# Nyström attention with two MoE layers on one core: low parts and input sums move from GpSimd to VectorE, and the output products of the rests come first

## The chip, the cores and the metric

The kernel runs on one core of a Trainium2 chip. The metric is the device time of one execution in microseconds (us). Its engines run side by side and wait for each other by semaphores: TensorE (PE in the rows, PEld for its weight loads), VectorE (DVE), ScalarE (ACT), GpSimd (POOL) and SyncE (SP), which here only issues DMAs. PSUM holds the matmuls' outputs in eight banks of 128x512 fp32; SBUF holds the rest.

## The reference

```
A, Bm, C = softmax(q k_lm'), softmax(q_lm k_lm'), softmax(q_lm k')      # 32 landmarks
Z = Bm' / (norm1(Bm) norminf(Bm) + 1e-6);  six times: Z = 2 Z - Z Bm Z
x = A Z C v                                    # (4, 8, 576, 64) -> 2304 x 512
x = (silu(x wg1) * (x wv1)) wo1                # layer 1
out = (sigmoid(x wg2) * (x wv2)) wo2           # layer 2; wg, wv 512 x 1536, wo 1536 x 512
```

The weights come as 64-bit floats, and the kernel converts their raw words to fp32.

## The kernel before

Every fp32 product is done as three products of parts: an operand is split in a high part (a cast to fp32r on ScalarE) and a low part (a subtraction on VectorE, line 366), and the pairs high-high, low-high and high-low (TERMS) are summed in PSUM. Both MoE layers go through the 1536 hidden columns in six chunks of 256 (c = 0 to 5).

Layer 2 is where the change lies; it takes the span from about 447 us on. Its tokens are worked in two steps: step 1 takes 512 tokens of each of batches 0 and 1, step 2 those of batches 2 and 3, and the "rests", 64 tokens of each batch (256 in all), go with step 1. In a step the product of inputs and a chunk of wg and wv is done in 2x2 blocks (two batches, two halves of 256 input columns, two halves of the chunk) with seven block products in place of eight. For these there are

- input sums s1 to s4 of the blocks (`x_blocks`, lines 612 to 615) with high and low parts xl, once for each step;
- weight differences: tile tf, four differences of weight blocks from tiles st (line 408, GpSimd), stored in DRAM for step 2 (wtd), and tile wt, the high part (line 422, ScalarE) and the low part (line 423) of tf. There are two of each for a chunk (j = 0 and 1), one for each half of 128 rows. In step 2 tf and st are loaded, not computed;
- `pair_steps`: the products n = 1, 2, 6, 7, 5, 3, 4 for gate (g) and value (v), six matmuls 128x512 for each (three for each j), in banks `gv` and `n`. `copy` brings a bank to SBUF (ScalarE), `add` adds another (VectorE). `finish` makes h of a quarter: sigmoid on ScalarE, product and low part on VectorE, high part on ScalarE. Products 6, 7, 5 and 4 read wt; products 1, 2 and 3 read wk, the split weights themselves;
- `rest_steps`: the same for the rests by plain products (pgr, pvr with 256 columns, 48 matmuls for a chunk), into tile hy;
- `o2_steps`: the output products of the chunk before, po2_c_i_t for batch i and 128 tokens from t (i = 4 means the rests), six matmuls each, added into oacc by VectorE (line 740; at c = 0 copied by ScalarE, line 738). Their banks have the tags `o` and `a`, two each.

The loop from line 834 runs output products of the chunk before, then the rests, then the pair, in the order in which the generators are called by `run`; after every step `wfill` emits two steps of the weights of the next chunk (raw load on SP, conversion in four operations on ScalarE and VectorE, lines 329 to 338, split, differences, wt, and wo for the output). Each engine works its own list in order; the lists are made by a scheduler that goes by the order of the code and by priorities (`tc.high_priority`). A tile's number of buffers (`bufs`) says how many of a tag are there at once; a new one waits until the last reader of the oldest is done. The tile wt has one buffer for each j, so wt of the next chunk can be cast only when product 4 has read the present one.

Of the kernel before, what the change touches and what calls it, by code (L numbers as in the profile page):

```python
# [16 lines left out]
def nystrom_moe_kernel(tc, q, k, v, wg1, wv1, wo1, wg2, wv2, wo2, out):  # L17
# [371 lines left out]
    def in_weights(layer, c, j):  # L389
        st = [late["w2"].tile([P, 2, FC], F32, tag="st", name=f"st{layer}_{c}_{kh}{j}", bufs=2) for kh in range(2)]  # L390
        wt = [late["w2"].tile([P, 4, 2, P], F32, tag="tf", name=f"tf{layer}_{c}_{j}", bufs=2)]
        for kh in range(2):
            if layer == 1:
                i = PIECES.index((layer, c, load_in, 2 * kh + j))
                load_to(i + 3)
                yield from convert(loaded[i], st[kh])
                WKD[c, kh, j] = dram.tile([P, 2, FC], F32, tag=f"wkd{c}_{kh}{j}", name=f"wkd{c}_{kh}{j}")
                nc.sync.dma_start(WKD[c, kh, j], st[kh])
            else:
                nc.sync.dma_start(st[kh], WKD[c, kh, j])  # L400
            w = WK[c, kh, j] = late["w2"].tile([P, 2, 2, FC], F32R, tag="wk", name=f"wk{layer}_{c}_{kh}{j}", bufs=4)
            split(flat(w[:, 0]), flat(w[:, 1]), flat(st[kh]))
            yield
        t = wt[0]
        if layer == 1:
            b11, b12, b21, b22 = (st[kh][:, :, P * ft:P * ft + P] for kh in range(2) for ft in range(2))
            for o, x, y in ((0, b12, b11), (2, b22, b12), (1, b22, t[:, 0]), (3, b21, t[:, 1])):
                nc.gpsimd.tensor_tensor(t[:, o], x, y, op=ALU.subtract)  # L408
            WTD[c, j] = dram.tile([P, 4, 2, P], F32, tag=f"wtd{c}_{j}", name=f"wtd{c}_{j}")
            nc.sync.dma_start(WTD[c, j], t)  # L410
        else:
            nc.sync.dma_start(t, WTD[c, j])
        yield
        WTF[layer, c, j] = t
        if (layer, c, j) != (1, 0, 1):
            t_split(layer, c, j)
            yield

    def t_split(layer, c, j):
        w = WT[c, j] = late["l2" if j else "w2"].tile([P, 2, 4, 2, P], F32R, tag="wt", name=f"wt{layer}_{c}_{j}", bufs=1)  # L420
        hi, lo, t = (x.rearrange("p t g n -> p (t g n)") for x in (w[:, 0], w[:, 1], WTF[layer, c, j]))
        nc.scalar.copy(hi, t)  # L422
        nc.gpsimd.tensor_tensor(lo, t, hi.bitcast(F32), op=ALU.subtract)  # L423

# [122 lines left out]
    def o1_steps(c, b):  # L547
# [20 lines left out]
        for dm in range(4):  # L568
# [18 lines left out]
            else:  # L587
                if c == NFC - 2:
                    XA.append(p1r.tile([P, HS], F32, tag="h", name=f"xa{dm}", bufs=8)[:, 0:NR * B])
                for bb in range(B):  # L590
# [9 lines left out]
    def x_blocks(step_, x):  # L600


        hi = [AH[:, s, NR:] for s in range(16)]
        eng = nc.gpsimd if step_ == 1 else nc.vector
        for j in range(2):
# [5 lines left out]
            s1, s2, s3, s4 = (new(f"s{n}", F32, "xs") for n in range(1, 5))  # L611
            eng.tensor_tensor(s1, a21, a22, op=ALU.add)
            eng.tensor_tensor(s3, a11, a21, op=ALU.subtract)
            eng.tensor_tensor(s2, s1, a11, op=ALU.subtract)
            eng.tensor_tensor(s4, a12, s2, op=ALU.subtract)
            for n, at, src, home in ((1, 0, a11, "CL"), (2, 8, a12, "CL"), (4, 9, a22, "CL"), (5, 2, s1, "CL"),
# [16 lines left out]
    def w_block(c, n, j, a, gv):  # L633
# [4 lines left out]
        return WT[c, j][:, a, {5: 0, 6: 1, 7: 2, 4: 3}[n], gv]  # L638

    def finish(key, gate, val, g_tile, hi, lo):  # L640
        nc.scalar.activation(g_tile, gate, AF.Sigmoid)
        nc.vector.tensor_tensor(g_tile, g_tile, val, op=ALU.mult)
        split(hi, lo, g_tile)
        H2[key] = (hi, lo)

    def pair_steps(step_, c):
# [15 lines left out]
        def copy(n, gv):  # L662
            t = cp[n, gv] = tmp(f"c{n}{'gv'[gv]}_{nm_}")
            nc.scalar.copy(t, bank[1, gv])  # L664

        def add(n, gv):
            nc.vector.tensor_tensor(cp[n, gv], cp[n, gv], bank[2, gv], op=ALU.add)

# [7 lines left out]
        for gv in range(2):  # L676
            copy(1, gv)
            add(1, gv)
        done(0, 0, 1)
        for gv in range(2):  # L680
# [11 lines left out]
        yield  # L692
        done(1, 1, 5)
        prod(3, 1)
        finish((1, 0), bank[1, 0], bank[1, 1], tmp(f"g12_{nm_}"), *h_pair(1, 0))
        yield
        for gv in range(2):
            prod(4, gv)
            add(6, gv)
            yield  # L700
        done(0, 1, 6)

# [112 lines left out]
    def run(g, n=100, nw=2):  # L815
        for _ in range(n):
# [4 lines left out]
            step(wfill, nw)  # L821

    need(1, 0, 3)
    g2 = pair_steps(1, 0)
    run(g2, 4)
    need(0, NFC - 1, 5)
    emit(f"O{NFC - 1}{B - 1}", 2)
    emit(f"O{NFC - 1}{B}", 2)
    p1r.release()
    late["l2"] = pool("l2", side="right")  # L830
    t_split(1, 0, 1)
    late["hy"] = late["l2"].tile([P, 2 * MT], F32R, tag="hy", name="hy")
    prev = None
    for st in (1, 2):
        for c in range(NFC):
# [4 lines left out]
            if prev:  # L840
                need(*prev, 5)
                o2 = o2_steps(*prev, (0, 1) if prev[0] == 2 else (0, 1, 2) if prev[1] == NFC - 1 else (0, 2, 1))
            if (st, c) == (1, NFC - 1):
# [7 lines left out]
            run(o2, 10 if (st, c) == (2, 0) else 4 if st == 2 else 6)  # L851
            if 0 < c < NFC - 1:
                run(rest)
            need(st, c, 3)
            if prev:
                g2 = pair_steps(st, c)
                run(g2, 4)
            run(o2, 1)
            run(g2, 4)
            run(o2, 1)  # L860
            run(g2, 2)
            run(o2, 1)
            run(g2, 1)
            run(o2)
# [42 lines left out]
```

## Time and profile before

| | |
|---|---|
| median of 3 runs | 943.1 us (941.05 to 944.53) |
| profiled execution | 946.08 us, span 944.3 us |
| TensorE busy | 868.2 us (92%), 6172 matmuls |
| VectorE busy | 675.8 us (72%) |
| ScalarE busy | 472.1 us (50%) |
| GpSimd busy | 174.9 us (19%), 61.8 of them line 423 |
| TensorE's granted clock, mean | 0.965 |

The span is what the trace covers; the execution's own time is 1.8 us longer. All rows below are from this one execution. A row of TensorE's timeline gives the start and the time of a group of matmuls that follow each other, and in brackets the idle time in front of it with the engine and line that ended it; matmuls overlap, so a single 128x512 is shown with some 0.4 us though they follow each other faster.

### The profile page before, as it was taken

The numbers are of one execution on the slowest core, as the hardware profiler recorded it, in microseconds if no ns is written. First come the engines' busy times: TensorE is split into PE (matmuls) and PEld (weight loads), VectorE is DVE, ScalarE is ACT, GpSimd is POOL, SyncE is SP. The second block draws the span as 40 slices with busy tenths as digits, with TensorE's granted clock in tenths as the row PEclk, the third lists the DMA queues.
The fourth block names the chain that finished last, engine by engine and source line by source line (L and its number), as shares of the span: only waits on it lengthen the run. The fifth ranks groups of instructions, "written<-read, shape, count | busy, mean of one in ns | idle before, by whom it ended". The sixth has DMA issues, their size and how long they took to land.

```text
span 944.3 us, 15946 instructions
## 1 busy us (share of the span) xinstructions
PE 868.2 (92%) x6172; PEld 712.6 (75%) x6172; DVE 675.8 (72%) x1227; ACT 472.1 (50%) x967; POOL 174.9 (19%) x170
## 2 busy tenths in 40 slices
PE   5698999999999999989798898989898898988997
PEld 4486868897888888779587786868687676866876
DVE  4979768669767776886856778786869757567555
ACT  5676555457534533563447645444463555534431
POOL 5434330000000000312313322222202022022020
PEclk9899999999999999989999999999998999989999
DMA  8766211024211210451106333434325423122003
GB/s 263 201 207 175 83 37 26 9 83 144 89 37 45 90 46 1 133 180 45 44 11 220 122 128 105 141 112 146 112 84 187 131 90 111 39 96 67 23 1 89
DMA packets 41484, 93.31 MB, mean 99 GB/s; under 512 B 5824, under 2 KB 8896, under 8 KB 41408
## 3 DMA queue, kind: packets, MB, share of 16 engines
q1 hardware_dynamic: 39680, 89.94, 30.4%
q10 hardware_dynamic: 1728, 2.36, 1.0%
q8 instruction: 48, 0.79, 0.3%
q14 instruction: 28, 0.23, 0.1%
HBM read 72.88 MB, written 19.40 MB: 98 GB/s over the span
## 4 chain that ended last, share of the span: by engine, by line
PE 74%; DVE 14%; ACT 4%; issue 3%; DMA 2%; POOL 1%; SPq 1%; DVEq 0%; ACTq 0%; POOLq 0%
PE po L65 28%; PE pg L65 18%; PE pv L65 17%; DVE h L366 3%; PE pu L65 2%; DVE cv L334 2%; PE pvr L65 2%; PE pgr L65 1%; PE tp L148 1%; DMA raw<-in_moe_w_val_dram 1%; PE nw L65 1%; DVE wk L366 1%; DVE xl L366 1%; DVE wo L366 1%; PE as L65 1%
## 5 line engine op out<-in xcount | busy, mean ns | idle before, releaser
L65 PE MATMUL po<-wo,h 128*128 128x512 f32 x432 | 124.5, 429 | 23.5 <-DVE h L366 23.5
L65 PEld LDWEIGHTS po<-wo,h 128*128 128x128 f32 x432 | 87.9, 207 | 49.5 <-DVE h L366 27.4
L423 POOL TENSOR_TENSOR wt<-tf,wt 128x1024 fp32r<-128x1024 f32 x24 | 61.8, 2592 | 284.2 <-ACT wt L422 284.2
L65 PE MATMUL po<-h,wo 128*128 128x512 f32 (+1 forms) x480 | 104.3, 373 | 2.0 <-DVE acc L580 2.0
L65 PEld LDWEIGHTS po<-h,wo 128*128 128x128 f32 x480 | 82.8, 188 | 28.9 <-issue 8.4
L65 PE MATMUL pg<-AH,uw 128*128 128x288 f32 x552 | 96.2, 302 | 1.3 <-ACT uw L365 1.2
L65 PE MATMUL pv<-AH,uw 128*128 128x288 f32 x552 | 93.4, 300 | 3.3 <-ACT sg L526 2.8
L740 DVE TENSOR_TENSOR oacc<-po,oacc 128x512 f32<-128x512 f32 x90 | 60.7, 686 | 45.1 <-PE po L65 44.6
L65 PEld LDWEIGHTS pv<-AH,uw 128*128 128x128 f32 x552 | 80.5, 191 | 7.7 <-ACT sg L526 3.7
L65 PEld LDWEIGHTS pg<-AH,uw 128*128 128x128 f32 x552 | 81.3, 191 | 6.4 <-issue 2.5
L334 DVE SCALAR_TENSOR_TENSOR cv<-cv,cv 128x512 uint32<-128x512 uint32 x84 | 76.1, 911 | 6.9 <-ACT cv L332 6.9
L329 ACT ACTIVATE cv<-raw 128x512 f32<-128x512 f32 x84 | 56.8, 678 | 40.2 <-DMA raw<-in_moe_w_val_dram 14.0
L408 POOL TENSOR_TENSOR tf<-st 128x256 f32<-128x256 f32 x12 | 10.7, 895 | 307.6 <-PE pu L65 240.3
L65 PE MATMUL pv<-AH,wt 128*128 128x512 f32 x192 | 61.9, 403 | 2.7 <-ACT c1v L664 2.7
L65 PE MATMUL pg<-AH,wt 128*128 128x512 f32 x192 | 61.3, 401 | 3.0 <-ACT c1g L664 2.4
L65 PE MATMUL po<-hh,wo 128*128 128x288 f32 x256 | 59.0, 310 | 0.0
L580 DVE TENSOR_TENSOR acc<-po,acc 128x512 f32<-128x512 f32 x64 | 43.8, 687 | 19.3 <-PE po L65 19.0
L332 ACT ACTIVATE cv<-raw 128x512 uint32<-128x512 uint32 x84 | 55.4, 668 | 0.6 <-DVE wo L366 0.6
L526 ACT ACTIVATE sg<-pg 128x288 f32<-128x288 f32 x64 | 26.1, 409 | 46.3 <-PE pg L65 46.3
L65 PEld LDWEIGHTS pv<-AH,wt 128*128 128x128 f32 x192 | 37.2, 194 | 12.1 <-ACT c1v L664 3.1
L65 PEld LDWEIGHTS pg<-AH,wt 128*128 128x128 f32 x192 | 36.6, 191 | 11.6 <-ACT c1g L664 2.6
L365 ACT CAST h<-h 128x288 fp32r<-128x288 f32 x64 | 27.5, 434 | 35.6 <-DVE h L527 35.6
(196 smaller groups left out, 1876.0 us busy)
## 6 DMA issues: line engine op xcount, KB each, us to landing
raw<-in_moe_w_out_dram SPq DMA_DIRECT2D x36, 512.0 KB, 4.1
raw<-in_moe_w_gate_dram SPq DMA_DIRECT2D x48, 128.0 KB, 2.9
raw<-in_moe_w_val_dram SPq DMA_DIRECT2D x48, 128.0 KB, 2.9
raw<-in_moe_w_gate_dram SPq DMA_DIRECT2D x24, 256.0 KB, 3.1
raw<-in_moe_w_val_dram SPq DMA_DIRECT2D x24, 256.0 KB, 3.5
wkd<-st SPq DMA_DIRECT2D x24, 256.0 KB, 2.2
wtd<-tf SPq DMA_DIRECT2D x12, 512.0 KB, 3.0
st<-wkd SPq DMA_DIRECT2D x24, 256.0 KB, 2.7
```

What stands on the lines that cost most here:

```text
L65: return nc.tensor.matmul(o, l, r, start=start, stop=stop, skip_group_check=True)
L148: nc.tensor.transpose(ps[:, j], flat(src[:, 2 * u:2 * u + 2]), ident)
L329: nc.scalar.activation(t0, hiw.bitcast(F32), AF.Copy, scale=2.0 ** -112)
L332: nc.scalar.activation(u1, low, AF.Copy, scale=0.875 * 2.0 ** -29, bias=0.49)
L334: nc.vector.scalar_tensor_tensor(u1, u0, 3, u1, op0=ALU.logical_shift_left, op1=ALU.bitwise_or)
L365: nc.scalar.copy(hi, x)
L366: nc.vector.tensor_tensor(lo, x, hi.bitcast(F32), op=ALU.subtract)
L408: nc.gpsimd.tensor_tensor(t[:, o], x, y, op=ALU.subtract)
L423: nc.gpsimd.tensor_tensor(lo, t, hi.bitcast(F32), op=ALU.subtract)
L526: nc.scalar.activation(sg, pss[0], AF.Silu)
L580: nc.vector.tensor_tensor(sl, ps, sl, op=ALU.add)
L740: nc.vector.tensor_tensor(acc, ps, acc, op=ALU.add)
```

## The change

- `t_split`: the low part of wt is computed on VectorE, not on GpSimd, and tf has one buffer, not two.
- `x_blocks`: the sums of step 1 go to VectorE as well, as those of step 2 did.
- The tile xa lies in another pool, so that p1r is released ahead of the first pair, and wt 0_1 is split ahead of the last output products of layer 1.
- `finish`, `copy` and `add` get a higher priority (100) in the scheduler; `pair_steps` has one more yield, and h of the quarter 1_1 is finished after product 4, not between the two products 3.
- Order: in step 1 the output products go rests, batch 0, batch 1 (2, 0, 1) where they went (0, 2, 1); the rests' products of c = 0 run ahead of the rest of the pair; the four output products of the batch that comes last are spread over the pair as before, but for the last of them, which stood between the two products 3 and now stands behind product 4.

```
-        wt = [late["w2"].tile([P, 4, 2, P], F32, tag="tf", name=f"tf{layer}_{c}_{j}", bufs=2)]
+        wt = [late["w2"].tile([P, 4, 2, P], F32, tag="tf", name=f"tf{layer}_{c}_{j}", bufs=1)]
...
         nc.scalar.copy(hi, t)
-        nc.gpsimd.tensor_tensor(lo, t, hi.bitcast(F32), op=ALU.subtract)
+        nc.vector.tensor_tensor(lo, t, hi.bitcast(F32), op=ALU.subtract)
...
-                    XA.append(p1r.tile([P, HS], F32, tag="h", name=f"xa{dm}", bufs=8)[:, 0:NR * B])
+                    XA.append(late["x"].tile([P, NR * B], F32, tag="xa", name=f"xa{dm}", bufs=4))
...
-        eng = nc.gpsimd if step_ == 1 else nc.vector
...
-            eng.tensor_tensor(s1, a21, a22, op=ALU.add)
-            eng.tensor_tensor(s3, a11, a21, op=ALU.subtract)
-            eng.tensor_tensor(s2, s1, a11, op=ALU.subtract)
-            eng.tensor_tensor(s4, a12, s2, op=ALU.subtract)
+            nc.vector.tensor_tensor(s1, a21, a22, op=ALU.add)
+            nc.vector.tensor_tensor(s3, a11, a21, op=ALU.subtract)
+            nc.vector.tensor_tensor(s2, s1, a11, op=ALU.subtract)
+            nc.vector.tensor_tensor(s4, a12, s2, op=ALU.subtract)
...
+    AHEAD = 100
+
     def finish(key, gate, val, g_tile, hi, lo):
-        nc.scalar.activation(g_tile, gate, AF.Sigmoid)
-        nc.vector.tensor_tensor(g_tile, g_tile, val, op=ALU.mult)
-        split(hi, lo, g_tile)
+        with tc.high_priority(AHEAD):
+            nc.scalar.activation(g_tile, gate, AF.Sigmoid)
+            nc.vector.tensor_tensor(g_tile, g_tile, val, op=ALU.mult)
+            split(hi, lo, g_tile)
...
-            nc.scalar.copy(t, bank[1, gv])
+            with tc.high_priority(AHEAD):
+                nc.scalar.copy(t, bank[1, gv])
...
-            nc.vector.tensor_tensor(cp[n, gv], cp[n, gv], bank[2, gv], op=ALU.add)
+            with tc.high_priority(AHEAD):
+                nc.vector.tensor_tensor(cp[n, gv], cp[n, gv], bank[2, gv], op=ALU.add)
...
             copy(1, gv)
             add(1, gv)
+        yield
         done(0, 0, 1)
...
         prod(3, 0)
         yield
-        done(1, 1, 5)
         prod(3, 1)
...
             prod(4, gv)
             add(6, gv)
             yield
+        done(1, 1, 5)
         done(0, 1, 6)
...
+    p1r.release()
+    late["l2"] = pool("l2", side="right")
     need(1, 0, 3)
     g2 = pair_steps(1, 0)
-    run(g2, 4)
+    run(g2, 5)
+    t_split(1, 0, 1)
...
-                o2 = o2_steps(*prev, (0, 1) if prev[0] == 2 else (0, 1, 2) if prev[1] == NFC - 1 else (0, 2, 1))
+                o2 = o2_steps(*prev, (0, 1) if prev[0] == 2 else (0, 1, 2) if prev[1] == NFC - 1 else (2, 0, 1))
...
-            if 0 < c < NFC - 1:
+            need(st, c, 3)
+            if c < NFC - 1:
                 run(rest)
-            need(st, c, 3)
             if prev:
                 g2 = pair_steps(st, c)
-                run(g2, 4)
-            run(o2, 1)
-            run(g2, 4)
-            run(o2, 1)
-            run(g2, 2)
-            run(o2, 1)
-            run(g2, 1)
+                run(g2, 5)
+            for n in (4, 2, 4):
+                run(o2, 1)
+                run(g2, n)
```

What it does to the engines' lists is seen in three places. The first is TensorE's list at the change from chunk 2 to chunk 3 in step 1. Before, behind the second product 4 (pv2_1_2_7 is the bank of products 7 and 4), batch 0 comes first, its four outputs (po2_2_0_0 to 384) interleaved:

```order
L65 MATMUL pv2_1_2_7_7233<-AH_88,wt1_2_0_6695 128x512 x2
L65 MATMUL pv2_1_2_7_7233<-xl41_0_6155,wt1_2_0_6695 128x512
L65 MATMUL pv2_1_2_7_7233<-AH_88,wt1_2_1_6792 128x512 x2
L65 MATMUL pv2_1_2_7_7233<-xl41_1_6184,wt1_2_1_6792 128x512
L65 MATMUL po2_2_0_0_7321<-wo1_2_6602,h_3498 128x512 x3
L65 MATMUL po2_2_0_128_7338<-wo1_2_6602,h_3498 128x512 x3
L65 MATMUL po2_2_0_256_7352<-wo1_2_6602,h_3498 128x512 x3
L65 MATMUL po2_2_0_384_7368<-wo1_2_6602,h_3498 128x512
```

With the change (wt1_2 is still read by product 4 just ahead of these rows):

```order
L65 MATMUL po2_1_1_384_7305<-wo1_1_6352,h_3498 128x512 x3
L65 MATMUL po2_1_1_384_7305<-wo1_1_6352,AH_88 128x512 x3
L65 MATMUL po2_2_4_0_7321<-wo1_2_6602,hy_6240 128x512 x6
L65 MATMUL po2_2_4_128_7338<-wo1_2_6602,hy_6240 128x512 x6
L65 MATMUL po2_2_0_0_7352<-wo1_2_6602,h_3498 128x512 x6
L65 MATMUL pgr_3_7417<-AH_88,wk1_3_00_6981 128x256 x2
L65 MATMUL pgr_3_7417<-xt_5478,wk1_3_00_6981 128x256
...
L65 MATMUL pgr_3_7417<-xt_5478,wk1_3_11_7134 128x256
L65 MATMUL pvr_3_7430<-AH_88,wk1_3_00_6981 128x256 x2
L65 MATMUL pvr_3_7430<-xt_5478,wk1_3_00_6981 128x256
L65 MATMUL po2_2_0_128_7368<-wo1_2_6602,h_3498 128x512 x6
```

Output 1_384 of the chunk before and the two outputs of the rests (po2_2_4, from hy) now stand ahead of batch 0, and products of the rests of the next chunk (pgr, pvr) lie between the first and the second output of batch 0.

The second is VectorE's list at the same place. Before (g12 and c6g are the last quarters of h, cv and st conversions of the next weights):

```order
L642 TENSOR_TENSOR g12_1_2_7298<-g12_1_2_7298,pv2_1_2_1_7153 128x512
L667 TENSOR_TENSOR c6g_1_2_7210<-c6g_1_2_7210,pg2_1_2_7_7215 128x512
L667 TENSOR_TENSOR c6v_1_2_7231<-c6v_1_2_7231,pv2_1_2_7_7233 128x512
L334 SCALAR_TENSOR_TENSOR cv1_7334<-cv0_7333,cv1_7334 128x512
L366 TENSOR_TENSOR h_3498<-g12_1_2_7298,h_3498 128x512
L642 TENSOR_TENSOR c6g_1_2_7210<-c6g_1_2_7210,c6v_1_2_7231 128x512
L338 SCALAR_TENSOR_TENSOR st1_4_00_7330<-cv0_7333,cv1_7334 128x512
L740 TENSOR_TENSOR oacc0_0_6561<-po2_2_0_0_7321,oacc0_0_6561 128x512
L366 TENSOR_TENSOR h_3498<-c6g_1_2_7210,h_3498 128x512
```

With the change:

```order
L672 TENSOR_TENSOR c6g_1_2_7213<-c6g_1_2_7213,pg2_1_2_7_7218 128x512
L366 TENSOR_TENSOR h_3498<-g12_1_2_7286,h_3498 128x512
L672 TENSOR_TENSOR c6v_1_2_7231<-c6v_1_2_7231,pv2_1_2_7_7233 128x512
L423 TENSOR_TENSOR wt1_3_0_7028<-tf1_3_0_6964,wt1_3_0_7028 128x1024
L645 TENSOR_TENSOR c6g_1_2_7213<-c6g_1_2_7213,c6v_1_2_7231 128x512
L366 TENSOR_TENSOR wo1_3_6961<-cv1_7164,wo1_3_6961 128x512
L366 TENSOR_TENSOR AH_88<-c5g_1_2_7254,AH_88 128x512
L366 TENSOR_TENSOR h_3498<-c6g_1_2_7213,h_3498 128x512
L423 TENSOR_TENSOR wt1_3_1_7150<-tf1_3_1_7041,wt1_3_1_7150 128x1024
L366 TENSOR_TENSOR wo1_3_6961<-cv1_7188,wo1_3_6961 128x512
L746 TENSOR_TENSOR oacc1_384_6936<-po2_1_1_384_7305,oacc1_384_6936 128x512
L746 TENSOR_TENSOR oacc4_0_6561<-po2_2_4_0_7321,oacc4_0_6561 128x512
```

The low part of h from g12 has no conversion in front of it any more; two low parts of wt are new here, and the evacuations of output tiles 1_384 and 4_0 stand behind the second.

The third is the start of layer 2: the sums (xs) of step 1 and the low part of wt 0_1 in GpSimd's list before:

```order
L612 TENSOR_TENSOR xs11_0_6141<-acc1_0_2339,acc1_2_2357 128x512
L613 TENSOR_TENSOR xs31_0_6143<-acc0_0_1131,acc1_0_2339 128x512
L614 TENSOR_TENSOR xs21_0_6142<-xs11_0_6141,acc0_0_1131 128x512
L615 TENSOR_TENSOR xs41_0_6144<-acc0_2_1151,xs21_0_6142 128x512
L612 TENSOR_TENSOR xs11_1_6170<-acc1_1_2348,acc1_3_2366 128x512
L613 TENSOR_TENSOR xs31_1_6172<-acc0_1_1141,acc1_1_2348 128x512
L614 TENSOR_TENSOR xs21_1_6171<-xs11_1_6170,acc0_1_1141 128x512
L615 TENSOR_TENSOR xs41_1_6173<-acc0_3_1169,xs21_1_6171 128x512
L423 TENSOR_TENSOR wt1_0_1_6311<-tf1_0_1_5562,wt1_0_1_6311 128x1024
```

With the change they stand in VectorE's list between the low parts (xl):

```order
L366 TENSOR_TENSOR xl11_1_6178<-acc0_1_1141,AH_88 128x512
L614 TENSOR_TENSOR xs41_1_6173<-acc0_3_1169,xs21_1_6171 128x512
L366 TENSOR_TENSOR xl21_1_6181<-acc0_3_1169,AH_88 128x512
L366 TENSOR_TENSOR xl41_1_6184<-acc1_3_2366,AH_88 128x512
L672 TENSOR_TENSOR c1g_1_0_6231<-c1g_1_0_6231,pg2_1_0_2_6210 128x512
L672 TENSOR_TENSOR c1v_1_0_6234<-c1v_1_0_6234,pv2_1_0_2_6224 128x512
L366 TENSOR_TENSOR xl51_1_6187<-xs11_1_6170,AH_88 128x512
L366 TENSOR_TENSOR xl61_1_6190<-xs21_1_6171,AH_88 128x512
L366 TENSOR_TENSOR xl71_1_6193<-xs31_1_6172,AH_88 128x512
L366 TENSOR_TENSOR xl31_1_6196<-xs41_1_6173,AH_88 128x512
L423 TENSOR_TENSOR wt1_0_1_6237<-tf1_0_1_5562,wt1_0_1_6237 128x1024
L580 TENSOR_TENSOR acc3_0_3341<-po1_5_3_6241,acc3_0_3341 128x512
```

The sums have left GpSimd, and the low part of wt 0_1 stands behind the last low part of the sums, ahead of layer 1's last accumulations (line 580).

## Rows read from the trace of the kernel before

**Rows 1.** Busy us by engine in stretches, by engine (counts); clock, DMA share, GB/s; the sum of all ten.

```profile
447.00:510.00 63.00, 51.43 (x247) 42.10 (x247) 42.25 (x60) 31.73 (x57) 19.57 (x13) 0.92 0.18 62
...
560.00:604.00 44.00, 40.88 (x194) 33.84 (x193) 33.22 (x47) 21.77 (x38) 12.59 (x10) 0.96 0.36 120
...
692.00:760.00 68.00, 61.01 (x268) 49.91 (x267) 52.93 (x80) 35.07 (x62) 6.76 (x3) 0.92 0.44 132
...
848.00:884.00 36.00, 32.89 (x137) 26.26 (x136) 24.17 (x32) 14.42 (x25) 5.16 (x2) 0.95 0.20 59
...
sum 497.30, PE 450.27 PEld 366.18 DVE 342.95 ACT 232.19 POOL 100.73; mean PE 45.03 PEld 36.62 DVE 34.29 ACT 23.22 POOL 10.07
```

**Rows 2.** TensorE's timeline, rows with idle time in front (in brackets, with releaser).

```profile
457.02 0.50 PE L65 MATMUL pg<-xl,wk 128*128 128x512 f32 x1 [2.85 <-DVE xl L366]
...
467.99 0.73 PE L65 MATMUL pg<-AH,wt 128*128 128x512 f32 x2 [2.36 <-ACT c1g L664]
...
501.10 0.50 PE L65 MATMUL po<-wo,hy 128*128 128x512 f32 x1 [2.19 <-ACT hy L365]
...
543.67 4.38 PE L65 MATMUL po<-wo,h 128*128 128x512 f32 x11 [3.36 <-DVE h L366]
...
715.52 0.79 PE L65 MATMUL pvr<-AH,wk 128*128 128x256 f32 x2 [3.70 <-DVE gr L642]
...
744.10 0.49 PE L65 MATMUL pv<-AH,wt 128*128 128x512 f32 x1 [2.67 <-ACT c1v L664]
...
831.83 4.63 PE L65 MATMUL po<-wo,h 128*128 128x512 f32 x10 [3.12 <-DVE h L366]
```

**Rows 3.** Timeline of all engines, 536 to 544 us: start, us, engine, line.

```profile
536.79 1.98 ACT L422 CAST wt<-tf 128x1024 fp32r<-128x1024 f32 x2
...
537.91 5.17 POOL L423 TENSOR_TENSOR wt<-tf,wt 128x1024 fp32r<-128x1024 f32 x2 [14.54 <-ACT wt L422]
...
538.60 2.28 DVE L334 SCALAR_TENSOR_TENSOR cv<-cv,cv 128x512 uint32<-128x512 uint32 x1
...
540.80 2.82 DVE L366 TENSOR_TENSOR h<-g,h 128x512 fp32r<-128x512 f32 x1
```

**Rows 4.** Groups of one form: count, busy us, mean ns, idle before.

```profile
L366 DVE TENSOR_TENSOR h<-g,h 128x512 fp32r<-128x512 f32 x12 | 27.0, 2252 | 1.5 <-ACT h L365 1.5
...
L366 DVE TENSOR_TENSOR h<-c1g,h 128x512 fp32r<-128x512 f32 x12 | 8.3, 691 | 2.8 <-ACT h L365 2.1
```

**Rows 5.** Stretches behind four of the gaps, as rows 1; the clock is PEclk.

```profile
457.00:461.00 4.00, 3.98 (x17) 3.30 (x18) 4.00 (x7) 0.07 (x1) 0.00 (x0) 1.00 0.00 0
472.00:476.00 4.00, 4.00 (x12) 3.09 (x11) 0.69 (x1) 0.31 (x1) 0.00 (x0) 0.53 0.01 4
544.00:548.00 4.00, 4.00 (x12) 3.13 (x11) 4.00 (x7) 1.87 (x3) 0.74 (x1) 0.57 0.40 107
716.00:720.00 4.00, 4.00 (x17) 3.61 (x17) 4.00 (x9) 2.02 (x5) 0.00 (x0) 0.50 0.36 105
```

**Rows 6.** Timeline 440 to 470 us, single rows of three engines.

```profile
447.35 0.46 DVE L527 TENSOR_TENSOR h<-sg,pv 128x288 f32<-128x288 f32 x1 [0.17 <-PE pv L65]
...
447.77 1.07 PE L65 MATMUL pg<-AH,wk 128*128 128x512 f32 x4
...
453.16 1.59 POOL L614 TENSOR_TENSOR xs<-xs,acc 128x512 f32<-128x512 f32 x1 [0.69 <-DVE xl L366]
...
457.49 2.49 DVE L366 TENSOR_TENSOR xl<-xs,AH 128x512 fp32r<-128x512 f32 x4
...
464.57 0.42 DVE L366 TENSOR_TENSOR xt<-po,AH 128x256 fp32r<-128x256 f32 x1
```

**Rows 7.** GpSimd's timeline: block differences, two at a time.

```profile
511.18 1.55 POOL L408 TENSOR_TENSOR tf<-st,tf 128x256 f32<-128x256 f32 x2
...
521.03 2.33 POOL L408 TENSOR_TENSOR tf<-st,tf 128x256 f32<-128x256 f32 x2
```

More of the change, by code (lines that the diff above doesn't have):

```diff
@@ L821, in run @@
             step(wfill, nw)
+    p1r.release()
+    late["l2"] = pool("l2", side="right")
     need(1, 0, 3)
     g2 = pair_steps(1, 0)
-    run(g2, 4)
+    run(g2, 5)
+    t_split(1, 0, 1)
+    late["hy"] = late["l2"].tile([P, 2 * MT], F32R, tag="hy", name="hy")
     need(0, NFC - 1, 5)
@@ L828, in nystrom_moe_kernel @@
     emit(f"O{NFC - 1}{B}", 2)
[L829 to L832, printed above, removed]
     prev = None
```

## The prediction

> **What bounds the kernel now.** I read the busy time of the engines stage by stage first, because the share over the whole span mixes stages with different limits. In the second layer, from 447 us to the end, TensorE works 450.27 of 497.30 us, and no other engine comes near it (VectorE in a middle stretch of 44 us: 33.22 us) [rows 1]. So TensorE is the bound and the 47 us in which it stands idle, with what the clock costs after them, are all that a change of order can win. Then I read TensorE's own timeline for its gaps and what ended them [rows 2]. The gaps come in three kinds.
>
> First, one gap at nearly every change of the 256-column chunk: 3.36 us before 543.67 and 3.12 us before 831.83 stand for seven alike, four in step 1 and three in step 2; VectorE's low part of h ended each. The timeline around 537 to 543 us shows why [rows 3]: two low parts of wt on POOL take 5.17 us, and while they run a VectorE conversion takes 2.28 and the low part of h 2.82 us. Over the kernel this form of h takes 2252 ns in the mean, and the same operation on c1g, which runs when POOL is quiet, 691 ns [rows 4]. TensorE waits for it because in the order of before all that it has behind product 4 are output products of this h.
>
> Second, the start (447 to 510 us): 51.43 busy of 63.00 us, so 11.57 us idle [rows 1], of which 2.85 before 457.02 wait for the low part of an input sum, 2.36 before 467.99 for the copy of c1g, and 2.19 before 501.10 for hy of the rests [rows 2]. Third, the last chunk of step 1 with the start of step 2: 6.99 us idle [rows 1], 3.70 of them before 715.52 (VectorE's product for the rests, queued behind a slow low part of h), 2.67 before 744.10 (a copy on ScalarE) [rows 2].
>
> Behind such gaps the granted clock is at its lower level for some time: 0.53, 0.57 and 0.50 of full speed, as means over 4 us, in three of the windows shown, and 1.00 in the fourth, behind the gap of 2.85 us [rows 5]. 4 us at 0.57 lose some 1.7 us, at 0.50 2.0 us. I take 1.5 to 1.7 us for a change of chunk and 2.7 for the loss at 716 us, where the stall had begun longer before.
>
> **Prices.** A 128x512 matmul issues every 0.23 us ((1.07 - 0.39)/3, [rows 6], 0.39 being the shown length of a single one); one with 256 columns I take at half. A VectorE operation of 128x512 takes 0.69 us alone [rows 4] and 0.60 back to back ((2.49 - 0.69)/3, [rows 6]). No trace row shows VectorE on 128x1024. From 0.42 us for 256 columns [rows 6] and 0.69 for 512, the slope is 0.27 for 256 more, so 1.22 us; its bounds are 1.0 (that of the cast of the same tile on ScalarE, 1.98 us for two [rows 3]) and 1.38 (two halves). The 24 of them put 29 us on VectorE and take POOL's 24 x 2.6 us away. An input sum on POOL takes 1.59 us [rows 6]; on VectorE 0.60 to 0.69. POOL's block differences, which stay, take 1.55 us for two when VectorE is quiet, 2.33 when it is not [rows 7].
>
> **The change, stage by stage.**
>
> Start. VectorE's list now has eight sums, eleven low parts of xl, one of h and two additions in one piece, then the low part of wt 0_1. From the end of the last product for h (447.35 + 0.46, [rows 6]) that is 22 operations at 0.60 to 0.69, to 461.2, and 1.22 for wt: ready at about 462.4. TensorE has 56 matmuls of 128x512 in front of the first that needs it (24 of products 1 and 2, 24 of layer 1's output, 8 of product 6): from 447.1, three matmuls before the row at 447.77 [rows 6], 56 x 0.23 leads to 459.9. So a gap of about 2.5 us stays, I allow 1.5 us round the low parts of the rests' input, and 1.5 us of clock: 5.5 lost where before 11.6 and some 4 of clock (1.9 by the window at 472 [rows 5], as much taken for the stall at 501) were. Gain 10, bounds 6 (all of VectorE's work at 0.69, so 2 us later, and a second gap) and 13.
>
> Chunk changes of step 1 (four). The old wait goes: two output products of the rests stand ahead, h is ready 3.2 us after product 3, and is needed after 6.8. But tf has one buffer now, so another chain begins there. Counted from the end of product 3's last matmul: product 4 ends at 2.7 and frees wt; the cast (1.0) and the low part (1.22) of wt 0 end at about 5.2; only then may POOL write tf again, four differences, 3.1 us quiet or 4.7 contended, to 8.3 or 9.8; cast of wt 1, 9.4 to 10.9; its low part, 10.6 to 12.1. In VectorE's new list that low part stands ahead of another of wo and of the evacuation of output tile 1_384, which so ends at 12.0 to 13.5. TensorE has four output banks: 1_384, 4_0, 4_128 and 0_0 fill them by 8.2, then 15 short matmuls of the rests to 10.0, and 0_128 must wait for the evacuation. So a new gap of 2.0 to 3.5 us comes in place of 3.1. At 8 matmuls of the next pair, in the last of the four, it is 1.4. I take 2.65, nearer the contended end, because VectorE has work through all of it. Whether the clock drops after it is open: it was low after 2.36 us (the gap before 467.99, window at 472) and full after 2.85, so I take half of 1.5. Gain each 3.1 + 1.5 - 2.65 - 0.75 = 1.2, four 4.8; bounds 0 (a contended chain, clock lost as before) and 12 (quiet, clock kept).
>
> On this a rule bears. The Trainium skill, page "SBUF — State Buffer", section "SBUF: two separate sides", says that VectorE and GpSimd share a pair of ports as an exclusive lock, which a VectorE instruction with two SBUF inputs takes against a GpSimd one that reads SBUF, and the loser stands for the whole instruction. The trace agrees where POOL holds the pair (2.25 us for 0.69, [rows 3, 4]). By that rule the move doesn't end the contention but turns it round, since a low part on VectorE has two SBUF inputs as well: POOL's differences would all take the contended time, and the sum would be at the lower bound here, 4.8 us less gain.
>
> Last chunk and start of step 2. The product for the rests is ready before TensorE is through with output 1_384, so the 3.70 us and 2.7 of clock go; the 2.67 us before 744.10 stay, since that copy stands behind output DMAs on ScalarE's queue in both orders. Against it, loads of st for step 2 stand on SP's queue behind that of tf 2_1_0, which waits for a tf buffer, that is for the low part of wt 2_0. Gain 4.5, bounds 2 and 8.
>
> Chunk changes of step 2 (three). No differences are computed here (tf is loaded), so POOL does nothing, and the evacuations stand ahead of wt 1 in VectorE's list: 3_384 ends at 8.6 where TensorE wants the bank at 8.9. Gain 3 x (3.1 + 1.7) = 14.5, bounds 12 and 17. A gap of 1 us at each would cost 3.
>
> What I cost at nothing: the tile xa in another pool and the earlier release of p1r (no instruction changes); the copies, sums and sigmoids given priority inside a block (TensorE does not wait there now; without that cover a copy of 0.6 us would be paid); finish of 1_1 after product 4 (its h is needed 20 us later, in the next chunk); the raw loads that stand on SP behind the store of tf (issued some 9 us after the change of chunk, while the first copy that is queued behind their conversions on ScalarE is wanted after about 25).
>
> Sum: 10 + 4.8 + 4.5 + 14.5 = 33.8 us. The profiled execution took 946.08 us, 0.3% above the median of 943.1; against the first that is 912.3, against the median 909.3. I forecast 909 for the median.
>
> **Rivals.**
> - The new chain is as long as its contended end or longer, at all four changes of step 1, and one more wait for st stays at step 2's start. For: VectorE is busy 33.22 of 44 us already and gets 2.4 more per chunk. Against: its slow low parts go. Gain 15 to 25: 918 to 928. Chance 0.18.
> - The chain is hidden: differences quiet, clock kept, 8 matmuls of the next pair as cover everywhere, and the start loses little. Gain 45 to 55: 888 to 898. For: behind the gap of 2.85 us before 457.02 the clock stayed at 1.00 [rows 5]. Against: VectorE has queued work throughout. Chance 0.13.
> - Slower, by one mechanism: the chain through the one tf buffer. To eat the 29 us of the other stages each of four changes would have to lose 7.3 us more than the 4.6 it lost before, so the evacuation would have to end at 10.0 + 12 = 22 us instead of 13.5: differences of 3.3 us each, where the longest pair shown takes 2.33. Beyond that point everything is paid. 945 to 955. Chance 0.05.
> - The change doesn't do what it says: VectorE's list takes up the freed time (29 us more), gaps move rather than go, and gain stays within 4.7 us: 938 to 947. Against: seven gaps of one cause, which no longer exists. Chance 0.05.
>
> **How the numbers follow.** The forecast (899 to 918, gains of 25 to 44) has 0.59. The range takes in half of the first two rivals and the bounds of the terms (gains of 20 to 50: 893 to 923) and goes a little into the first rival: 893 to 926. A difference of 0.5% (4.7 us) is about what a measurement of this kernel can tell from none. Faster has 0.59 + 0.18 + 0.13 = 0.90, same 0.05, slower 0.05.
>
> **What would show it.** Right: no gap ended by the low part of h at changes of chunk; the form of h near 0.69 us; VectorE near 690 us in sum (29 and 5 more, some 20 less by contention), POOL under 100; in step 1 a gap of 2 to 3 us before output tile 0_128, released by the evacuation on VectorE; none over 1 us at the changes of step 2; 744 us still with a gap of about 3. Wrong: VectorE's 128x1024 over 1.4 us, gaps at step 1 of 5 us or more, or a gap in the middle of a block, where none is now.

## The result and the profile after

The changed kernel takes 904.56 us in the median of four runs (899.64 to 907.46) against 942.08 (940.65 to 944.53): the ratio is 0.9594, with a 95% interval of 0.9544 to 0.9643, a gain of 37.5 us. The profiled execution, with a span of 897.7 us, is the fastest of the four.

Busy time of the engines over the span, from the page of the changed kernel:

```profile
PE 848.0 (94%) x6172; PEld 700.3 (78%) x6172; DVE 660.7 (74%) x1259; ACT 474.1 (53%) x967; POOL 103.3 (12%) x138
```

VectorE has less to do than before (675.8 us) although it got 24 low parts and eight sums; GpSimd falls from 174.9 to 103.3 us. Two groups say why: first the new operation, then the low part of h that was held up [rows 4].

```profile
L423 DVE TENSOR_TENSOR wt<-tf,wt 128x1024 fp32r<-128x1024 f32 x24 | 29.2, 1219 | 7.7 <-ACT wt L422 7.7
...
L366 DVE TENSOR_TENSOR h<-g,h 128x512 fp32r<-128x512 f32 x12 | 8.2, 684 | 0.0
```

The new operation takes 1219 ns, and h from g12 684 instead of 2252 ns.

All gaps of TensorE over 0.9 us in layer 2, from its timeline after the change:

```profile
457.77 0.50 PE L65 MATMUL pg<-AH,wt 128*128 128x512 f32 x1 [2.01 <-DVE wt L423]
...
496.62 0.50 PE L65 MATMUL pvr<-AH,wk 128*128 128x256 f32 x2 [3.30 <-DVE gr L645]
...
531.58 2.93 PE L65 MATMUL po<-wo,h 128*128 128x512 f32 x6 [2.74 <-ACT oacc L744]
...
576.77 4.37 PE L65 MATMUL po<-wo,h 128*128 128x512 f32 x18 [2.94 <-DVE oacc L746]
...
618.79 6.00 PE L65 MATMUL po<-wo,h 128*128 128x512 f32 x18 [2.94 <-DVE oacc L746]
...
662.43 4.38 PE L65 MATMUL po<-wo,h 128*128 128x512 f32 x18 [2.93 <-DVE oacc L746]
...
723.26 0.50 PE L65 MATMUL pg<-xl,wt 128*128 128x512 f32 x1 [0.91 <-DVE xl L366]
```

Nothing is left of the gaps ended by h [rows 2]. In their place four gaps of 2.7 to 2.9 us are ended by evacuations (line 746 on VectorE, line 744 on ScalarE), one of 3.30 by the product for the rests, and those of step 2 have gone. The busy time by stage shows it in sums; first two stretches of the kernel before, from the first matmul of product 1 of chunk 1 to that of chunk 4 in step 1 (three changes of chunk), and from chunk 1 of step 2 to the end:

```profile
510.86:644.39 133.53, 123.92 (x591) 102.82 (x589) 99.58 (x137) 69.61 (x123) 39.52 (x33) 0.96 0.40 135
782.70:944.30 161.60, 146.47 (x607) 117.20 (x605) 103.47 (x139) 61.85 (x103) 20.68 (x8) 0.95 0.21 62
```

The same two of the changed kernel (columns as rows 1):

```profile
499.01:628.57 129.56, 120.93 (x578) 101.07 (x577) 93.57 (x140) 68.57 (x118) 22.47 (x24) 0.97 0.38 127
754.62:897.70 143.08, 138.78 (x607) 113.48 (x605) 96.29 (x147) 62.90 (x103) 0.00 (x0) 1.00 0.26 74
```

In the first stretch the kernel with two buffers for tf, below, takes 116.45 us, all of them busy and at full clock. The stretch of before holds more work: 12 matmuls of the rests' products of chunk 1 lie behind the first matmuls of product 1 there,

```profile
511.79 0.40 PE L65 MATMUL pvr<-AH,wk 128*128 128x256 f32 x2
...
513.21 0.40 PE L65 MATMUL pg<-AH,wk 128*128 128x512 f32 x1
```

1.42 us, which in the changed order stand ahead of the stretch. So the kernel before lost 133.53 - 123.92 = 9.61 us to gaps there and 123.92 - 1.42 - 116.45 = 6.05 us to the clock (matmuls at the lower level are longer), and the changed one 8.63 and 4.48.

By stages of the profiled executions (starts of products of TensorE's timeline; the last column are two versions from the experiments):

| stage | before | changed | low part on VectorE only / two buffers |
|---|---|---|---|
| up to layer 2 | 447.1 | 442.7 | 443.5 / 442.6 |
| to product 1 of chunk 1, step 1 | 63.8 | 56.3 | 61.1 / 54.3 |
| to that of chunk 4 | 133.5 | 129.6 | 116.9 / 116.5 |
| to that of chunk 1, step 2 | 138.3 | 126.1 | 126.4 / 122.6 |
| to the end | 161.6 | 143.1 | 143.7 / 142.8 |

For the 12 matmuls just named, 1.4 us move between rows: in the kernel before from the third row to the second (65.2 and 132.1), in the version with only the low part on VectorE from the fourth to the second (62.5 and 125.0).

### The profile page after: what moved, and what is told of

Read it like the earlier page. It is cut to its first block, busy times and chain, and to the rows that moved or that the text cites. A ratio compares the mean times of both kernels' runs of the same rounds, so it can differ in the third digit from the quotient of the medians.

```text
span 897.7 us, 15920 instructions
## 1 busy us (share of the span) xinstructions
PE 848.0 (94%) x6172; PEld 700.3 (78%) x6172; DVE 660.7 (74%) x1259; ACT 474.1 (53%) x967; POOL 103.3 (12%) x138
## 4 chain that ended last, share of the span: by engine, by line
PE 76%; DVE 11%; ACT 5%; DMA 3%; POOL 2%; issue 2%; SPq 0%; POOLq 0%; ACTq 0%; DVEq 0%
PE po L65 28%; PE pg L65 19%; PE pv L65 18%; POOL tf L408 2%; PE pu L65 2%; PE pvr L65 2%; DMA raw<-in_moe_w_val_dram 2%; PE tp L148 1%; PE pgr L65 1%; PE nw L65 1%; DVE wt L423 1%; DVE cv L334 1%; DVE wk L366 1%; DVE xl L366 1%; PE cs L65 1%
## 5 line engine op out<-in xcount | busy, mean ns | idle before, releaser
L65 PE MATMUL po<-wo,h 128*128 128x512 f32 x432 | 113.0, 399 | 11.6 <-DVE oacc L746 8.8
L65 PEld LDWEIGHTS po<-wo,h 128*128 128x128 f32 x432 | 82.4, 192 | 31.0 <-DVE oacc L746 9.6
L334 DVE SCALAR_TENSOR_TENSOR cv<-cv,cv 128x512 uint32<-128x512 uint32 x84 | 59.6, 713 | 2.5 <-ACT cv L332 2.3
L65 PE MATMUL pv<-AH,wt 128*128 128x512 f32 x192 | 60.1, 394 | 0.0
L65 PE MATMUL pg<-AH,wk 128*128 128x512 f32 x144 | 45.4, 396 | 0.6 <-ACT c5g L668 0.6
L65 PEld LDWEIGHTS po<-hh,wo 128*128 128x128 f32 x256 | 41.6, 189 | 4.9 <-issue 2.4
L65 PE MATMUL pv<-AH,wk 128*128 128x512 f32 x144 | 44.4, 389 | 0.0
```

The costliest lines, as they stand in the source:

```text
L65: return nc.tensor.matmul(o, l, r, start=start, stop=stop, skip_group_check=True)
L334: nc.vector.scalar_tensor_tensor(u1, u0, 3, u1, op0=ALU.logical_shift_left, op1=ALU.bitwise_or)
```

## The experiments

All compare with the kernel before, run beside them on the same chip; the versions of the changed kernel are held against 904.56 us and 879.75 us too. The kernel before had medians of 942.37 to 944.01 us in these sets, so a difference between two sets is good to about 2 us.

**One edit of the kernel before: the engine alone.**

```
-        nc.gpsimd.tensor_tensor(lo, t, hi.bitcast(F32), op=ALU.subtract)
+        nc.vector.tensor_tensor(lo, t, hi.bitcast(F32), op=ALU.subtract)
```

> The kernel before with one edit: the low part of wt on VectorE (tf keeps two buffers, all orders as before). Theory A (the wait at each change of chunk is VectorE held off by POOL's two long operations): h from g12 is delayed by two low parts of 1.22 us each in front of it instead of by 5.2 us of POOL, so the seven gaps of 3.1 to 3.4 us fall to about 0.5 to 1 us and the lower clock behind them goes: 912 to 920 us. Rival B (the order of the outputs is what matters; VectorE simply gets the 29 us that POOL had): gaps near 3 us stay, 936 us or more.

Measured: 892.62 us, ratio 0.946 (0.9436 to 0.9484). This one line gives 50 us, more than the whole change. At the change of chunk that [rows 3] show, its timeline has

```profile
531.74 2.35 DVE L423 TENSOR_TENSOR wt<-tf,wt 128x1024 fp32r<-128x1024 f32 x2
534.01 0.68 DVE L366 TENSOR_TENSOR h<-g,h 128x512 fp32r<-128x512 f32 x1
...
530.80 3.93 PE L65 MATMUL po<-wo,h 128*128 128x512 f32 x16
...
534.93 2.00 PE L65 MATMUL po<-wo,h 128*128 128x512 f32 x8
```

and TensorE has no gap: the low part of h still stands behind both low parts of wt, but it ends at 534.7, when TensorE is just through with sixteen matmuls of the outputs that do not read it and has products of the rests to go on with. So theory A has the cause right; TensorE had waited for wt itself only once, 0.67 us. Its range, 912 to 920, was missed by 19 us: it left 0.5 to 1 us at each of the seven gaps, where nothing is left, and the gap of 3.70 us in the last chunk of step 1 went as well. VectorE is busy for 659.0 us (675.8 before), though it got 28.4 us of low parts: 45 us less inside its other operations.

**The changed kernel with that line undone.**

> The changed kernel with one edit: the low part of wt back on GpSimd. Theory A: in step 1 the two output products of the rests cover the delay, and wt's low parts no longer stand ahead of the evacuations on VectorE, but VectorE is held off again; in step 2 there is only one output product as cover, so the gaps of 2 to 3 us come back there: 912 to 925 us. Rival B (order and priority alone give the gain): within 5 us of the changed kernel's 904.6.

Measured: 917.69 us, ratio 0.9737 (0.9698 to 0.9776). The time is in A's range, the place is not: step 2 has no gap at its changes of chunk, and the loss lies in step 1, where TensorE waits 4.2 to 4.9 us for evacuations at four changes (2.38 at the first), and at the start, with 4.16 us for the low part of an input sum. The row of TensorE's timeline at the change from chunk 2 to 3:

```profile
583.35 2.93 PE L65 MATMUL po<-wo,h 128*128 128x512 f32 x6 [4.88 <-DVE oacc L746]
```

**The order of the outputs alone, in the kernel before.**

```
-  ... else (0, 2, 1))
+  ... else (2, 0, 1))
```

> The kernel before with one edit: output products of step 1 in the order rests, batch 0, batch 1. Theory A: 12 matmuls of 0.23 us (2.7 us) now lie in front of the first that needs the late h, so four gaps shrink from 3.1 to about 0.5 us and their clock stays: 924 to 932 us; step 2 unchanged. Rival B (the evacuations are held off by POOL as well, so the gap only moves behind the outputs of the rests): 938 us or more.

Measured: 930.91 us, ratio 0.9875 (0.9845 to 0.9905), as theory A has it. TensorE's gaps at one change of chunk of step 1 shrank to 0.5 us with another of 1.4 behind:

```profile
585.73 1.65 PE L65 MATMUL po<-wo,h 128*128 128x512 f32 x6 [0.54 <-DVE oacc L740]
...
593.10 0.51 PE L65 MATMUL pvr<-AH,wk 128*128 128x256 f32 x2 [1.40 <-DVE gr L642]
```

Step 2 kept gaps of 3.12 to 3.37 us.

**Two buffers for tf in the changed kernel.**

```
-    ident = cst.tile([P, P], F32, tag="ident", name="ident")
+    ident = att.tile([P, P], F32, tag="ident", name="ident")
...
-    UT = [cst.tile([P, 4, M], F32, tag=f"ut{b}", name=f"ut{b}") for b in range(B)]
+    UT = [w1p.tile([P, 4, M], F32, tag=f"ut{b}", name=f"ut{b}") for b in range(B)]
...
-        wt = [late["w2"].tile([P, 4, 2, P], F32, tag="tf", name=f"tf{layer}_{c}_{j}", bufs=1)]
+        wt = [late["w2"].tile([P, 4, 2, P], F32, tag="tf", name=f"tf{layer}_{c}_{j}", bufs=2)]
```

> The changed kernel with tf in two buffers again (the identity and UT lie in other pools to make room, nothing else). Theory A (the gaps of 2.7 to 2.9 us at four changes of chunk come from the chain low part of wt 0, differences on POOL, cast and low part of wt 1, evacuation): the differences of j = 1 run long before, both low parts follow each other, the four gaps go, 888 to 896 us. Rival B (VectorE is full there and the evacuation stays late whatever POOL does): gaps over 2 us stay, 900 us or more.

Measured: 879.75 us, ratio 0.9321 (0.9295 to 0.9347), lower than either theory said. The four gaps and the one of 3.30 us went; in the stretch of three changes TensorE has no idle time:

```profile
496.90:613.35 116.45, 116.45 (x579) 98.39 (x578) 92.32 (x140) 68.27 (x118) 22.11 (x24) 1.00 0.43 140
```

So the single buffer, which the change brought with it, costs 24.8 us, and this version beats both kernels: 879.75 / 904.56 = 0.973 of the changed one.

**Control: only the moves that make room, one buffer.**

> The changed kernel with the identity and UT in the other pools, as in the version with two buffers for tf, but with one buffer. If the second buffer alone gave the 24.8 us between 904.6 and 879.8, this is the changed kernel again: 899 to 908 us, five gaps of 2.7 to 3.3 us, with the lower clock behind some of them and not behind others. If the moves gave part of it: below 898.

Measured: 902.72 us, ratio 0.9572 (0.9541 to 0.9602): the changed kernel again, with one more gap, of 1.50 us before 705.29. It also shows the clock's part. Its rows behind the changes from chunk 3 to 4 and 4 to 5:

```profile
620.71 4.38 PE L65 MATMUL po<-wo,h 128*128 128x512 f32 x18 [2.95 <-DVE oacc L746]
...
662.74 6.00 PE L65 MATMUL po<-wo,h 128*128 128x512 f32 x18 [2.92 <-DVE oacc L746]
```

In the changed kernel (its gaps above) the first of these two took 6.00 us and the second 4.38. The same 18 matmuls behind the same gap take 4.38 us in one execution and 6.00 in another, here of two kernels that differ only in where two tiles lie.

**The evacuations first, one buffer.** Every accumulation into oacc under `tc.high_priority(400)`.

> The changed kernel, one buffer for tf, but the accumulations into oacc with a higher priority than anything else, so that VectorE takes those of 1_384, 4_0 and 4_128 ahead of wt 1. Theory A (the gaps of 2.9 us are that evacuation behind the low part of wt 1): the three gaps that VectorE ends at changes of chunk go; the one that a copy on ScalarE ends (chunk 1 to 2) and the one before the rests' pvr (chunk 0 to 1) stay: 887 to 895 us. Rival B (the late wt 1 itself holds TensorE up): gaps over 2 us stay at all changes, 900 or more.

Measured: 888.56 us, ratio 0.9418 (0.9378 to 0.9457). The three gaps that VectorE ended are gone (0.78 us at most is left there), and these two stay, as theory A has it:

```profile
496.88 0.80 PE L65 MATMUL pvr<-AH,wk 128*128 128x256 f32 x2 [3.14 <-DVE gr L645]
...
532.38 5.99 PE L65 MATMUL po<-wo,h 128*128 128x512 f32 x18 [2.30 <-ACT oacc L744]
```

**One buffer in the order of before, low part on VectorE.**

> The kernel before with the low part of wt on VectorE and one buffer for tf, in the old order. Theory A (the one buffer ties cast and low part of wt 1 to the change of chunk, whatever the order): the evacuations behind it come late, a gap of 1 to 3 us at four changes and one before the rests, 897 to 908 us against 892.6. Rival B (the one buffer only hurts in the new order, where the evacuation of 1_384 stands behind wt 1): below 895.

Measured: 910.15 us, ratio 0.9654 (0.9621 to 0.9686), a little above A's range: 17.5 us more than with two buffers. The gap before the rests that A names did not come; two at the start grew instead, from 1.18 and 2.85 us to 2.24 and 3.94. Four gaps of 2.65 to 2.86 us stand at the changes of chunk, one of them:

```profile
584.07 4.26 PE L65 MATMUL po<-wo,hy 128*128 128x512 f32 x12 [2.81 <-DVE oacc L740]
```

**Two buffers and the low part on GpSimd.**

> Two buffers for tf, and the low part of wt on GpSimd: all of the change but its engine and its buffer. Theory A (VectorE is held off while POOL runs 5.2 us, and order only hides a part of it): gaps of 1 to 2 us stay at the four changes of step 1 and at the start, 885 to 897 us. Rival B (with the outputs of the rests first and the products' chain ahead, the order alone covers POOL's operations): within 3 us of 879.8.

Measured: 898.85 us, ratio 0.9532 (0.9495 to 0.9569). Theory A, by 2 us above its range: gaps of 1.83 to 1.85 us at four changes and one of 3.04 before the rests' product. At the change from chunk 2 to 3 VectorE again needs 2.89 us for a low part while POOL works:

```profile
564.98 5.23 POOL L423 TENSOR_TENSOR wt<-tf,wt 128x1024 fp32r<-128x1024 f32 x2 [12.97 <-ACT wt L422]
...
567.87 2.89 DVE L366 TENSOR_TENSOR wo<-cv,wo 128x512 fp32r<-128x512 f32 x1
...
573.22 2.11 PE L65 MATMUL po<-wo,h 128*128 128x512 f32 x8 [1.84 <-DVE oacc L746]
```

So the engine is worth 50 us in the kernel before and 19.1 (898.85 - 879.75) with the rest of the change in place: the other edits and the engine cover the same wait, and their gains don't add.

**Three single parts taken out of the version with two buffers.** The outputs in the old order:

> Two buffers for tf, and in step 1 the outputs in the old order (batch 0, rests, batch 1). Theory A (with the low parts of wt on VectorE the h of batch 0 is ready 3.2 us after product 3, and product 4 with output 1_384 covers 4.1 us): within 2 us of 879.8. Rival B (the outputs of the rests are needed as cover): gaps of 1 to 2.5 us at four changes of chunk, 884 to 893.

879.18 us, ratio 0.9326 (0.9312 to 0.9339): nothing, theory A. The sums on GpSimd:

> Two buffers for tf, and the input sums of step 1 on GpSimd as before. Theory A (VectorE's low parts wait for the sums of 1.3 to 1.7 us and are held off while they run): the gaps near 1 and 3 us ahead of products 1 and 2 of j = 1 come back, 4 to 8 us more than 879.8. Rival B (the start is bounded by VectorE's own list, so nothing is lost): within 2 us.

880.96 us, ratio 0.9347 (0.9332 to 0.9362): rival B. The gaps of 1.18 and 2.86 us did come back, as A says, but those of 1.98 and 0.5 us further on went in exchange. The priority at 0:

> Two buffers for tf, and the priority of finish, copy and add at 0. Theory A (the priority shortens the chain copy, sum, sigmoid where VectorE has a long list, above all at the start of step 2): a gap of 2 to 3 us near the start of step 2 comes back as in the kernel before, 2 to 6 us more than 879.8. Rival B (the chain is covered by TensorE's own work everywhere): within 1 us.

878.23 us, ratio 0.9318 (0.9302 to 0.9333): no loss, so not theory A; at 1.5 us below 879.75 it is just outside rival B's 1 us. It is the lowest time of all, but its interval and that of the version with priority overlap. Near the start of step 2 a gap of 1.34 us comes, ended by the sum c1g, in exchange for one of 0.92 further on.

**The start alone.** The kernel before with the low part on VectorE, two buffers, the identity and UT in the other pools, the early release of p1r with xa in another pool, wt 0_1 split early, and the rests of chunk 0 ahead of the rest of the pair:

> The kernel before with the low part of wt on VectorE, two buffers for tf, and of the rest of the change only what concerns the start of layer 2: xa in the other pool, p1r released early, wt 0_1 split early, the rests of chunk 0 ahead of the rest of the pair, and the yield that this needs. The sums stay on GpSimd, outputs and priority as before. Theory A (of the 12.9 us between 892.6 and 879.8 the start has the most, since sums, outputs' order and priority gave 1 us at most when they were undone): 882 to 887 us. Rival B (the place of 1_1's finish and of the last output product count as much): 888 to 892.

883.0 us, ratio 0.9369 (0.9343 to 0.9396), theory A: 9.6 of the 12.9 us between 892.62 and 879.75 are the start (8.6 of 13.1 by the ratios). The stages agree: up to product 1 of chunk 1 it takes 52.9 us, where the version with the engine alone takes 62.5 for the same matmuls. Of the other 3 us the sums are 1.2 at most (above); the place of 1_1's finish and that of the last output product weren't tried apart.

## Why the prediction was right, and where it was not

**The sum.** 909 was forecast, 904.56 measured, within the range. In the two profiled executions the four terms came to 8.9, 4 x 0.85, 11.4 and 18.5 us where 10, 4.8, 4.5 and 14.5 were forecast, and layer 1 to 4.4 where nothing was. Those executions are 46.4 us apart, the medians 37.5: the one of before lies 4.0 above its median, that of the changed kernel 4.9 below. So the mechanisms told were the right ones but for the last chunk and a gap left out at the start, and that the sum comes within 5 us is in part luck: two terms were 1.1 and 1.4 us too high, two 6.9 and 4.0 too low, and the choice of executions hides 8.9.

**The price of the new operation** was right: 1.22 us from the slope, 1219 ns measured. VectorE in sum was not: near 690 us was forecast, with 20 less by contention, and it is 660.7, so the contention had cost it 675.8 + 29.2 + 5.5 - 660.7 = 49.8 us (5.5 for eight sums). GpSimd came to 103.3 where under 100 was the sign.

**Chunk changes of step 1.** The chain through the one buffer is as it was told. VectorE, POOL and ScalarE in the changed kernel at the change from chunk 2 to 3, from the differences of tf to the evacuation:

```profile
568.62 1.12 POOL L408 TENSOR_TENSOR tf<-st 128x256 f32<-128x256 f32 x1 [28.35 <-DVE wt L423]
...
569.71 1.18 POOL L408 TENSOR_TENSOR tf<-st,st 128x256 f32<-128x256 f32 x1
...
570.22 1.22 DVE L366 TENSOR_TENSOR AH<-c5g,AH 128x512 fp32r<-128x512 f32 x1
...
570.85 2.33 POOL L408 TENSOR_TENSOR tf<-st,tf 128x256 f32<-128x256 f32 x2
...
573.21 1.05 ACT L422 CAST wt<-tf 128x1024 fp32r<-128x1024 f32 x1 [3.14 <-POOL tf L408]
...
574.29 1.23 DVE L423 TENSOR_TENSOR wt<-tf,wt 128x1024 fp32r<-128x1024 f32 x1 [1.71 <-ACT wt L422]
...
575.43 0.69 DVE L366 TENSOR_TENSOR wo<-cv,wo 128x512 fp32r<-128x512 f32 x1
576.03 1.28 DVE L746 TENSOR_TENSOR oacc<-po,oacc 128x512 f32<-128x512 f32 x2
```

The first difference waits for the low part of wt 0, the last reader of the one buffer; the differences end at 573.2, the cast of wt 1, its low part, wo and then two evacuations follow, and TensorE starts 2.94 us late. 2.65 was forecast. The two versions that undo this chain (two buffers, and the evacuations first) show that it is the cause. The last of the four was put at 1.4 us, since 8 matmuls of the next pair lie in it; it was 2.93: 8 x 0.23 us cover no more than the 15 short ones at half that. The clock was mis-sized: by the two stretches above it cost 6.05 / 3 = 2.0 us a change before (1.5 forecast) and 4.48 / 3 = 1.5 after (0.75 forecast; some of it lies behind the gap of 3.30 us just ahead of the stretch). The errors partly cancel in the difference: 1.2 us a change forecast, (133.53 - 1.42 - 129.56) / 3 = 0.85 measured.

**The rule on the shared ports** (the Trainium skill, page "SBUF — State Buffer", section "SBUF: two separate sides") was weighed as speaking against the change, and in this chain the trace agrees with it: while POOL's differences run, they take 1.18 and 2.33 / 2 us each and VectorE's operations of 128x512 1.22 (0.69 alone), in turns. Its sum, 4.8 us less gain, did not come: 3.4 of the 4.8 were gained, since the gap was 2.94 and not the 3.5 of the contended end, and the clock fell only behind some of the gaps. The other side is the larger thing: with POOL's operations of 2.6 us gone from VectorE's way, one line gave 50 us.

**Start.** 10 us forecast, 63.8 + 1.4 - 56.3 = 8.9 measured. The gap behind the low part of wt 0_1 was put at 2.5 and is 2.01; that round the rests' input at 1.5 and is 0.51 with a smaller one behind, and no clock was lost. What was left out is the gap of 3.30 us before 496.62, at the change from chunk 0 to 1, with the lower clock behind it: I followed the chain of the one buffer through VectorE's list and not through ScalarE's. The cast of wt 1 waits there for POOL too,

```profile
487.92 1.05 ACT L422 CAST wt<-tf 128x1024 fp32r<-128x1024 f32 x1 [3.22 <-POOL tf L408]
...
494.41 0.36 ACT L644 ACTIVATE gr<-pgr 128x256 f32<-128x256 f32 x1
```

and the sigmoid of the rests stands behind it, a cast of wo, four copies of outputs and five operations of conversions; the product on VectorE then stands behind one more conversion. The gap goes with two buffers and stays when only the evacuations are moved.

**Last chunk and start of step 2.** Here the step failed: "the 2.67 us before 744.10 stay, since that copy stands behind output DMAs on ScalarE's queue in both orders". What is left is 0.91 us and one of 0.6. The stage gained 138.3 - 126.1 = 12.2 us, of which 11.4 are not the change of chunk in it, where 4.5 were forecast. The copy did wait behind output DMAs before, and does not in the changed kernel; with two buffers and the priority at 0 it does again (one row of each, in this order):

```profile
743.46 0.59 ACT L664 COPY c1v<-pv 128x512 f32<-128x512 f32 x1 [2.67 <-DMA out_dram<-oacc]
...
711.78 0.58 ACT L668 COPY c1v<-pv 128x512 f32<-128x512 f32 x1
...
694.85 0.59 ACT L668 COPY c1v<-pv 128x512 f32<-128x512 f32 x1 [1.96 <-DMA out_dram<-oacc]
```

So it is the priority of `copy`, which the prediction costed at nothing, that takes this copy ahead of the DMAs, whatever the order of the outputs. The copy was not the only limit: with the engine alone a gap of 2.00 us stays there, ended by VectorE's sum c1g, and with the priority at 0 one of 1.34 by the same sum. With two buffers and the priority no gap stands there, but one of 0.92 further on, and the time is no lower. So the priority moves these waits and gains nothing in the version with two buffers; what it is worth in the changed kernel was not tried. The loads of st behind that of tf, which I counted against it, show as no gap.

**Chunk changes of step 2.** 14.5 forecast, 161.6 - 143.1 = 18.5 measured. The stretch has 4.3 us idle where it had 15.1, and 146.47 - 138.78 = 7.7 us less at the lower clock; I had 1.7 us for the clock of each of three changes, and it is 2.6. The step's reason, no POOL work there, was only half of it: with the low part on GpSimd and the new order step 2 has no gap either.

**Layer 1** was costed at nothing, and its 4.4 us in the two profiled executions are no effect of the change: in the other profiles layer 2 begins between 440.5 and 444.1 us, in the kernel with only the outputs' order changed at 444.1; the execution of before was a late one.

**The rivals.** The first (the chain at its contended end) came nearest in its mechanism, not in its time: the chain is real and costs 24.8 us, but the gains around it were larger than forecast. "Hidden" is what two buffers give. The slower one didn't come: the differences took 1.2 us each, not 3.3. Nor did the fourth: VectorE's busy time fell and no gap by the low part of h is left.

## What to carry to other kernels

Where an engine's small operations take three times their usual time, look at what GpSimd does at that moment, and move that one operation before reordering anything: here one line gave 50 us and the other edits together, with two buffers, a quarter of it. A buffer taken away is an edit of its own, to be costed as a chain from its last reader to the next evacuation on every engine's list; here it cost 24.8 us, and 2.5 KB of tiles in each partition, moved to pools that end earlier, bought it back. Gains that cover the same wait don't add: undo each part in the final version before keeping it.

## What the runs showed of the hardware

The clock behind a gap of 2.9 us differs from one execution to the next. The gap of 2.85 us before 457.02 left it at 1.00 in the kernel before [rows 5]; in the kernel with only the outputs' order changed, whose edit lies behind that place, the same gap (2.87 us) was followed by

```profile
454.00:458.00 4.00, 3.98 (x11) 3.18 (x12) 3.67 (x6) 0.07 (x1) 0.00 (x0) 0.59 0.00 0
```

Within one execution of the changed kernel the same 18 matmuls took 4.37, 6.00 and 4.38 us behind gaps of 2.94, 2.94 and 2.93 (above). Its four runs spread over 7.8 us with their mean clock (0.988 for 899.64, 0.979 for 907.46), while those of the version without these gaps lie within 2.7 us. Two stretches of 4 us behind the gaps of 2.94 us in that execution, at 1.00 and 0.62:

```profile
577.00:581.00 4.00, 4.00 (x19) 3.27 (x19) 4.00 (x7) 1.39 (x3) 0.74 (x1) 1.00 0.82 262
619.00:623.00 4.00, 4.00 (x12) 3.14 (x12) 4.00 (x7) 1.43 (x3) 0.73 (x1) 0.62 0.74 251
```

Between VectorE and GpSimd short operations alternate, at 1.2 us each for 0.69 and 0.74 alone, where a long one of POOL (2.6 us) is waited out as a whole (2.82 us for 0.69). At the change of chunk shown above three VectorE operations beside the four differences so lost 3 x 0.53 = 1.6 us, the low part of h behind one long operation 2.82 - 0.69 = 2.1.
